# Even fold's row on GpSimd and ScalarE, earlier folds, V's and the norm's parts at other steps, and a first up product inside the attention loop

## The chip, the cores and the metric

One core of one Trainium2 chip. The metric is device time in microseconds (us) from one launch to its end. Matrix products run on TensorE (PE), the rest on VectorE (DVE), ScalarE (ACT) and GpSimd (POOL); SyncE (SP) issues nearly all transfers. Each engine works through its own queue in order and waits on semaphores for the others.

## The reference

Three blocks in a row, two batches of 768 tokens, float32:

```python
# 1: cluster attention: 8 heads of 64 per batch
mask = argmax(q_n . c_n)[:, None] == argmax(k_n . c_n)[None, :]
scores = where(mask, q @ k.T / 8, -1e9)
x = softmax(scores) @ v                      # heads side by side: 768 x 512
# 2: Fourier mixing, norm, MLP
u = x + real(fft(fft(x, axis=tokens), axis=features))
un = (u - mean(u)) / sqrt(var(u) + 1e-6)
x = u + relu(un @ w_ch1) @ w_ch2             # 512 -> 2048 -> 512
# 3: gated convolution MLP
h = relu(x @ w_in)                           # 512 -> 1024
out = (h * sigmoid(conv3(h))) @ w_out
```

## The kernel before, in words

Products keep float32 accuracy by splitting each operand into a high and a low part and multiplying three times (`pass3`).

**Attention.** 16 pairs of batch and head are cut into 6 blocks of 128 queries, 96 blocks in all. One loop runs over the step n from -8 to 105 (L791 to 815). At step n it issues, in this order: what the dictionary `pre` holds for n; the s products of block n+8 and, on VectorE, their maximum (`score_max`, L552 to 571), with `mid` between the two; the high part of block n-1's probabilities (`prob_hi`); the t products of block n and their exponential on ScalarE (`score_exp`); the low part of n-1 (`prob_lo`), on VectorE for the blocks in `LO_ON_DVE`, else on GpSimd; the products of block n-3 with V (`attn_v`); then `aft`, `post` and `fill`. `at(where, n, f)` puts further work into these five. The order of this loop is written by hand (`manual_schedule`): every engine's queue holds exactly the sequence that the steps issue. From block 88 on the odd blocks (`IN_PLACE`) keep their probabilities in PSUM.

Score tiles are three slots of two PSUM banks in rotation (`slot`, L356). A product waits until the slot's last reader is done, most often the maximum, the exponential, or an in-place low part.

For a pair m of heads (8 pairs) `prep_*` picks clusters and builds stacked operands (its 24 cluster products, `prep_sims`, are issued at step 12m-19), and `v_*` scales V: `load_v` (a transfer into the one tile `vraw`), `v_max` (magnitude, VectorE), `v_turn` (a product that turns it), `v_step` 0 to 3 (small, VectorE), 4 (scaled copy, ScalarE) and 5 (the residual, VectorE).

Inside the loop run also, for batch 0: the mixing (`mixing`, table `plan` L702 to 709), whose even fold adds mirrored halves (`even0`, `even1`), takes a row of 257 differences on one partition (`row`, L131 to 137, into rows 0 and 32 of `Zx`), then sums and splits (`even`, `evenH`, `evenL`); the norm (`norm`, L713 to 720), six token tiles in five parts each; conversions of two weight blocks ahead (`ahead_*`); and the split of the first weight block (`first_split`).

**MLPs.** After the loop the program is no longer ordered by hand: a planner sorts each engine's queue by the readiness that it computes, and may draw such work into the loop's idle time. `mlp1_up(0, 0)` is the first up product, of 2 halves with 12 products each; `load_w` brings a weight block as 64-bit words (tile `raw64`, two buffers) and converts it with four VectorE operations and one of ScalarE (`from64`); `squares` sums squares of a block on ScalarE and overwrites its raw tile, for blocks 0 and 1 in two `junk` tiles of the same two buffers. `later` issues batch 1's mixing as a side line of the first MLP.

Of the kernel before, what the change touches and what calls it, by code (L numbers as in the profile page):

```python
# [24 lines left out]
LO_ON_DVE = ({n for n in range(54) if n % 12 in (2, 7, 8, 10)}  # L25
             | {n for n in range(54, 87) if n % 12 in (1, 2, 7, 11)} | {87})

# [22 lines left out]
def tile_net(ctx, tc, qk, v, cen, w12, w34, conv, dft, odd, out):  # L50
# [3 lines left out]
    def f32(ap):  # L54
        return ap.bitcast(F32)
# [39 lines left out]
    def mixing(b, bank, bank2, low, other):  # L95
# [35 lines left out]
        @stage("row")  # L131
        def _():
            r1 = dp.tile([1, N2], F32, tag="row", bufs=1, name=f"r1{b}")
            ev = d["ev", 0], d["ev", 1]
            V.tensor_sub(r1[:, 0:257], ev[0][0:1, 0, 0:257], ev[1][0:1, 0, 0:257])
            V.tensor_copy(Zx[0:1, 0:257], r1[:, 0:257])
            V.tensor_sub(Zx[32:33, 0:257], r1[:, 0:257], f32(Zx[0:1, 0:257]))

# [173 lines left out]
    def load_w(k, f):  # L312
        w = place_w(k, f)
        raw = cvs[0].tile([128, 2048], I32, tag="raw64", bufs=2, name=f"raw{k}{f}")
        nc.sync.dma_start(out=raw.bitcast(I64), in_=(w12 if k == "a" else w34)[f])
        for op in from64(w, raw):
            op()
        squares(k, f, raw[:, 0:256].bitcast(BF16))

# [28 lines left out]
    with ExitStack() as actx:  # L348
# [7 lines left out]
        def slot(name):  # L356
            turn[0] = (turn[0] + 1) % 3
            return ps.tile([128, 2, 512], F32, tag=f"s{turn[0]}", bufs=1, name=name)
# [301 lines left out]
        def at(where, step, *f):  # L660
            where.setdefault(step, []).append(f)

        for m in range(1, NH // 2):
            k = 12 * m - 24
            if m > 1:
                at(pre, k, load_raw, m)
                at(post, k + 5, prep_sims, m)
                at(fill, k + 6, prep_first, m)
                at(fill, k + 7, prep_pick, m)
                at(fill, k + 8, prep_hi, m, (0,))  # L670
                at(fill, k + 9, prep_lo, m, 0, G)
                at(fill, k + (9 if m < 7 else 8), prep_hi, m, (1,))
                at(mid, k + 11, prep_turn, m)
                at(fill, k + (10 if m < 7 else 9), prep_lo, m, 1, G)
            at(fill, k + 14, load_v, m)
            at(aft, k + 17, v_max, m)
            at(mid, k + 19, v_turn, m)
            for i in range(4):
                at(aft, k + 19, v_step, m, i)
            at(fill, k + 24, v_step, m, 4)  # L680
            at(fill, k + 25, v_step, m, 5)
        at(fill, -8, prep_first, 1)
# [3 lines left out]
        at(fill, 0, stack_mask, 2)  # L686
        at(fill, 0, v_step, 0, 5)
        at(pre, -2, first_max, 0)
# [8 lines left out]
        def two(name):  # L697
# [3 lines left out]
        first = mixing(0, lambda name: slot(name)[:, 0], two, V, G)  # L701
        plan = (("even0", fill, 54), ("even1", fill, 55), ("row", aft, 57), ("even", fill, 58), ("evenH", aft, 59),  # L702
                ("evenL", fill, 59),
                ("odd0", fill, 60), ("y0", post, 61), ("odd1", fill, 61), ("y0L", pre, 62), ("y1", post, 62),
# [9 lines left out]
        for i, t in enumerate((0, 3, 1, 4, 2, 5)):  # L714
            n = 73 + 3 * i
            at(fill, n, stat, t)
            at(pre, n + 1, root, t)
            at(aft, n + 2, scale, t)
            at(post, n + 3, swap, t)
            at(pre, n + 4, low, t)  # L720

# [19 lines left out]
        for i, t in enumerate((Zx, Zy, YcH[:, :, N1:512], YcL[:, :, N1:512])):  # L741
            at(fill, 4 + i, V.memset, f32(t), 0.0)
        for q in range(AHEAD):
            at(pre, AHEAD_STEPS[5 * q] - 3, ahead_start, q)
            at(pre, AHEAD_STEPS[5 * q + 4] + 1, ahead_store, q)
# [12 lines left out]

        at(fill, 92, first_split, 0)
        at(fill, 93, first_split, 1)  # L760
        at(fill, 95, first_split, 2)
        at(fill, 97, first_split, 3)

# [92 lines left out]
    def mlp1_up(g, f):  # L856
        if (g, f) == (0, 0):
            h = hs[0, g, f] = [dp.tile([128, 780], F32R, tag=t, bufs=1, name=f"first{t}")[:, 0:S] for t in ("e0", "e1")]
            w = ws[0, g, f]
        else:  # L860
            if g:
                t = hp.tile([128, S], F32R, tag="hH", bufs=3, name=f"h{g}_{f}").bitcast(F16)
                h = hs[0, g, f] = [t[:, 0:S], t[:, S:2 * S]]
                w = ws[0, g, f] = split_16(hp, "a", f) if f == 0 else ws[0, g, f]
            else:
                h = hs[0, g, f] = [hp.tile([128, S], F32R, tag=t, bufs=3, name=f"{t}{g}_{f}") for t in ("hH", "hL")]
                w = ws[0, g, f] = split_w(hp, 3, "a", f, f"a{g}_{f}", V)
        for i in range(2):
# [145 lines left out]
    side = later()  # L1014
    mlp1_up(0, 0)
    for f in range(2):
        squares("a", f, cvs[0].tile([128, 2048], I32, tag="raw64", bufs=2, name=f"junk{f}")[:, 0:256].bitcast(BF16))
    load_w("a", 2)
# [110 lines left out]
```

## Time and profile before

| | us |
|---|---|
| median of 3 runs | 701.67 (700.02 to 703.91) |
| profiled execution, its span | 702.69, 700.9 |
| PE busy | 667.3 (95%) |
| DVE busy | 543.9 (78%) |
| ACT busy | 410.8 (59%) |
| POOL busy | 200.3 (29%) |

The profile is of one execution, so a sum made from its rows is to be compared with 702.69. A busy PE is not PE at its peak: matmuls overlap, and a lower granted clock makes each longer. The attention loop fills the span from 15 to 282 us; the first MLP follows, then the second.

### The profile page before, as it was taken

What the parts mean: (1) busy time and instruction counts of PE and PEld (TensorE: products, weight loads), DVE (VectorE), ACT (ScalarE), POOL (GpSimd) and SP (SyncE); (2) the same over time, 40 slices, a digit from 0 to 9 for tenths busy, and PEclk for the clock granted to TensorE, in tenths of its full rate; (3) what the DMA queues carried; (4) which work ended last, traced back from release to release, by engine and by line L of the source; (5) the groups of instructions that cost most, each with busy time, mean ns of one, the idle gap of its engine ahead of it and who ended that gap; (6) DMA issues with size and microseconds to landing.
All of it is one profiled execution on the core that took longest, in us unless ns stands there. A gap on an engine that the chain in (4) does not pass through costs nothing.

```text
span 700.9 us, 12789 instructions
## 1 busy us (share of the span) xinstructions
PE 667.3 (95%) x5106; PEld 504.6 (72%) x5106; DVE 543.9 (78%) x873; ACT 410.8 (59%) x664; POOL 200.3 (29%) x168
## 2 busy tenths in 40 slices
PE   8799999998899997989999999999999999999997
PEld 6598988987799886869998998555555555555553
DVE  7777889898877997999469976997634399867662
ACT  3478869787458787536335654676534367555442
POOL 8156658568646945121041000000000000000000
PEclk9999999999899999999999999999999999999999
DMA  7747696773633413224203350243000000001002
GB/s 219 198 110 193 158 244 157 213 209 84 155 87 78 106 62 122 68 98 144 113 0 121 121 180 10 77 156 122 0 2 1 1 0 1 1 1 71 20 1 90
DMA packets 22087, 66.50 MB, mean 95 GB/s; under 512 B 4502, under 2 KB 7562, under 8 KB 19212
## 3 DMA queue, kind: packets, MB, share of 16 engines
q1 hardware_dynamic: 21020, 61.94, 31.0%
q0 software_dynamic: 1008, 3.75, 2.0%
q8 instruction: 40, 0.66, 0.4%
q14 instruction: 19, 0.16, 0.1%
HBM read 40.94 MB, written 5.77 MB: 67 GB/s over the span
## 4 chain that ended last, share of the span: by engine, by line
PE 72%; DVE 16%; DMA 4%; issue 2%; ACT 2%; POOL 2%; SPq 1%; DVEq 0%; ACTq 0%; POOLq 0%
PE acc L86 8%; PE acc L87 8%; PE acc L85 8%; PE up L85 5%; PE up L87 5%; PE up L86 5%; PE av L641 5%; PE s L566 3%; PE t L601 3%; PE s L568 3%; PE t L603 3%; DVE m L571 3%; PE sim L440 3%; PE u L85 2%; PE u L87 2%
## 5 line engine op out<-in xcount | busy, mean ns | idle before, releaser
L629 POOL TENSOR_TENSOR p<-p,p 128x768 f16<-128x768 f32 x62 | 107.5, 1735 | 85.7 <-ACT p L621 59.5
L571 DVE TENSOR_REDUCE m<-s 128x1 f32<-128x768 f32 x96 | 90.5, 947 | 13.8 <-PE s L568 6.5
L609 ACT ACTIVATE p<-t,cbias 128x768 f32<-128x768 f32 x92 | 82.8, 900 | 26.2 <-PE t L603 25.0
L621 ACT CAST p<-p 128x768 f16<-128x768 f32 x88 | 73.0, 830 | 1.2
L641 PE MATMUL av<-V,p 128*128 128x65 f16 x1728 | 70.8, 195 | 2.8 <-POOL p L629 2.8
L641 PEld LDWEIGHTS <-p 128*128 128x128 f16 x1728 | 59.3, 99 | 18.3 <-issue 15.1
L601 PE MATMUL t<-X 128*128 128x384 f32 x192 | 54.5, 365 | 8.6 <-DVE m L571 6.9
L566 PE MATMUL s<-X 128*128 128x384 f32 x192 | 56.2, 374 | 3.2 <-DMA X<-ohd 1.8
L568 PE MATMUL s<-Y 96*128 96x384 f32 x192 | 50.0, 341 | 1.1 <-DMA Y<-G 1.1
L603 PE MATMUL t<-Y 98*128 98x384 f32 x192 | 50.2, 343 | 0.0
L85 PE MATMUL up<-un,wha 128*128 128x384 f32 x120 | 41.3, 344 | 2.7 <-DVE YcL L163 1.3
L85 PE MATMUL u<-x,wb 128*128 128x384 f16 x128 | 41.7, 326 | 1.3 <-DVE h L892 0.9
L87 PE MATMUL up<-un,wla 128*128 128x384 f32 x120 | 40.5, 338 | 1.8 <-DVE wla L853 1.8
L601 PEld LDWEIGHTS t<-X 128*128 128x128 f32 x192 | 32.0, 192 | 13.9 <-issue 6.7
L85 PE MATMUL up<-un,wa 128*128 128x384 f16 x128 | 41.7, 326 | 0.0
L87 PE MATMUL up<-un,wa 128*128 128x384 f16 x128 | 41.7, 326 | 0.0
L86 PE MATMUL up<-un,wa 128*128 128x384 f16 x128 | 41.7, 326 | 0.0
L87 PE MATMUL u<-x,wb 128*128 128x384 f16 x128 | 41.7, 326 | 0.0
L86 PE MATMUL u<-x,wb 128*128 128x384 f16 x128 | 41.7, 326 | 0.0
L86 PE MATMUL up<-un,wha 128*128 128x384 f32 x120 | 40.5, 338 | 0.0
L629 DVE TENSOR_TENSOR p<-p,p 128x768 f16<-128x768 f32 x30 | 37.7, 1257 | 0.1
L85 PE MATMUL acc<-wb,gH 128*128 128x512 f16 x96 | 36.4, 379 | 0.5 <-ACT gH L900 0.5
(368 smaller groups left out, 1701.0 us busy)
## 6 DMA issues: line engine op xcount, KB each, us to landing
rawa<-w SPq DMA_DIRECT2D x14, 1024.0 KB
rawb<-w SPq DMA_DIRECT2D x8, 1024.0 KB
raw<-qk SPq DMA_DIRECT2D x7, 768.0 KB
X<-G SPq DMA_DIRECT2D x14, 384.0 KB
Y<-G SPq DMA_DIRECT2D x14, 384.0 KB
vraw<-v SPq DMA_DIRECT2D x8, 384.0 KB
out<-y SPq DMA_DIRECT2D x12, 256.0 KB
X<-G SPq DMA_DIRECT2D x14, 192.0 KB
```

Of the source, the lines that this page charges most:

```text
L85: T.matmul(o, sH, mH, start=start, stop=False)
L86: T.matmul(o, sH, mL, start=False, stop=False)
L87: T.matmul(o, sL, mH, start=False, stop=stop)
L566: T.matmul(t[:, c, 0:384], X[:, 0, sl], X[:, 1, 384 * c:384 * c + 384], start=True, stop=False)
L568: T.matmul(t[:, c, 0:384], Y[0:96, 0, sl], Y[0:96, 1, 384 * c:384 * c + 384], start=False, stop=True)
L571: V.tensor_reduce(m6s[h][:, i:i + 1], t[:, :, 0:384], AX.XY, ALU.max, negate=True)
L601: T.matmul(t[:, c, 0:384], X[:, 1, sl], X[:, 0, 384 * c:384 * c + 384], start=True, stop=False)
L603: T.matmul(t[:, c, 0:384], Y[0:98, 1, sl], Y[0:98, 0, 384 * c:384 * c + 384], start=False, stop=True)
L609: A.activation(p, t[:, :, 0:384], AF.Exp, bias=cbias, scale=0.125)
L621: A.copy(p16[:, 0], p32s[n])
L629: eng.tensor_sub(p16[:, 1], p, p16[:, 0])
L641: T.matmul(o, p16[:, k, 128 * j:128 * j + 128], v16[:, i, h % 2, 65 * part:65 * part + 65], start=(i + j + k + part == 0), stop=(i == 5), ...
```

## The change

- `row` is four stages: a subtraction on GpSimd, a copy on ScalarE (`rowH`), a second subtraction on GpSimd (`rowL`), a copy on ScalarE (`rowZ`). In batch 0 they stand at steps 54, 56, 56 and 58; `even0` and `even1` move from 54 and 55 to 52 and 53. In batch 1 they follow each other.
- V's parts of pair m: the load at 12m-17 (before 12m-10), the magnitude at 12m-12 (12m-7), its turn and the small steps at 12m-10 (12m-5), the scaled copy and the residual at 12m-7 (12m and 12m+1), the step that issues the next pair's cluster products. The first pair's stand at 0, 4, 5 and 5, the last pair's copy and residual at 78 and 79.
- The norm's five parts all move one step later.
- `first_split` is at 91 to 94 (92 to 97). The first up product is issued at steps 96 and 97 in two halves, from slots of the loop, ahead of the products of blocks 94 and 95 with V.
- The low part of block 94 moves to VectorE.
- The squares of weight blocks 0 and 1 are taken with those of blocks 4 and 5, over their raw tiles.

```diff
-             | {n for n in range(54, 87) if n % 12 in (1, 2, 7, 11)} | {87})
+             | {n for n in range(54, 87) if n % 12 in (1, 2, 7, 11)} | {87, 94})
...
         @stage("row")
         def _():
-            r1 = dp.tile([1, N2], F32, tag="row", bufs=1, name=f"r1{b}")
-            ev = d["ev", 0], d["ev", 1]
-            V.tensor_sub(r1[:, 0:257], ev[0][0:1, 0, 0:257], ev[1][0:1, 0, 0:257])
-            V.tensor_copy(Zx[0:1, 0:257], r1[:, 0:257])
-            V.tensor_sub(Zx[32:33, 0:257], r1[:, 0:257], f32(Zx[0:1, 0:257]))
+            r1 = d["r1"] = dp.tile([1, N2], F32, tag="row", bufs=1, name=f"r1{b}")
+            G.tensor_sub(r1[:, 0:257], d["ev", 0][0:1, 0, 0:257], d["ev", 1][0:1, 0, 0:257])
+        @stage("rowH")
+        def _():
+            A.copy(Zx[0:1, 0:257], d["r1"][:, 0:257])
+        @stage("rowL")
+        def _():
+            G.tensor_sub(d["r1"][:, 0:257], d["r1"][:, 0:257], f32(Zx[0:1, 0:257]))
+        @stage("rowZ")
+        def _():
+            A.copy(Zx[32:33, 0:257], d["r1"][:, 0:257])
...
-        squares(k, f, raw[:, 0:256].bitcast(BF16))
+        for i in (f, f - 4) if k == "a" and f in (4, 5) else (f,):
+            squares(k, i, raw[:, 0:256].bitcast(BF16))
...
-            at(fill, k + 14, load_v, m)
-            at(aft, k + 17, v_max, m)
-            at(mid, k + 19, v_turn, m)
+            first = m == 1
+            at(fill, 0 if first else k + 7, load_v, m)
+            at(aft, 4 if first else k + 12, v_max, m)
+            at(mid, 5 if first else k + 14, v_turn, m)
             for i in range(4):
-                at(aft, k + 19, v_step, m, i)
-            at(fill, k + 24, v_step, m, 4)
-            at(fill, k + 25, v_step, m, 5)
+                at(aft, 5 if first else k + 14, v_step, m, i)
+            at(aft, k + 17 + (m == 7), v_step, m, 4)
...
-        at(fill, 0, v_step, 0, 5)
+        fill[0].insert(0, (v_step, 0, 5))
...
-        plan = (("even0", fill, 54), ("even1", fill, 55), ("row", aft, 57), ("even", fill, 58), ("evenH", aft, 59),
-                ("evenL", fill, 59),
+        plan = (("even0", fill, 52), ("even1", fill, 53), ("row", fill, 54), ("rowH", aft, 56), ("rowL", fill, 56),
+                ("even", fill, 58), ("rowZ", fill, 58), ("evenH", aft, 59), ("evenL", fill, 59),
...
-            at(fill, n, stat, t)
+            at(fill, n + 1, stat, t)
...
+        for m in range(1, NH // 2):
+            at(aft, 12 * m - 7 + 2 * (m == 7), v_step, m, 5)
...
+        def first_up(i):
+            if i == 0:
+                hs[0, 0, 0] = [dp.tile([128, 780], F32R, tag=t, bufs=1, name=f"first{t}")[:, 0:S] for t in ("e0", "e1")]
+            h, tk = hs[0, 0, 0], slice(384 * i, 384 * i + 384)
+            o = slot(f"up0_{i}")[:, 0, 0:384]
+            up_half(o, ws[0, 0, 0], uns[0], i)
+            A.activation(h[0][:, tk], o, AF.Relu)
+            V.scalar_tensor_tensor(h[1][:, tk], o, 0.0, f32(h[0][:, tk]), ALU.max, ALU.subtract)
-        at(fill, 92, first_split, 0)
-        at(fill, 93, first_split, 1)
-        at(fill, 95, first_split, 2)
-        at(fill, 97, first_split, 3)
+        at(fill, 91, first_split, 0)
+        at(fill, 92, first_split, 1)
+        at(fill, 93, first_split, 2)
+        at(fill, 94, first_split, 3)
+        at(post, 96, first_up, 0)
+        at(post, 97, first_up, 1)
...
-    mlp1_up(0, 0)
-    for f in range(2):
-        squares("a", f, cvs[0].tile([128, 2048], I32, tag="raw64", bufs=2, name=f"junk{f}")[:, 0:256].bitcast(BF16))
     load_w("a", 2)
```

## Rows read from the trace of the kernel before

**Rows 1.** The page's first part: engine, busy us, share, instructions.
```profile
PE 667.3 (95%) x5106; PEld 504.6 (72%) x5106; DVE 543.9 (78%) x873; ACT 410.8 (59%) x664; POOL 200.3 (29%) x168
```

**Rows 2.** Timeline at block 59: start us, us, engine, line, operation, shapes [idle before <-releaser].
```profile
169.49 1.85 POOL L115 TENSOR_TENSOR ev<-U 128x765 f32<-128x765 f32 x1
...
171.37 1.85 DVE L135 TENSOR_TENSOR r<-ev,ev 1x257 f32<-1x257 f32 x1 [1.13 <-POOL ev L115]
...
175.06 1.74 DVE L137 TENSOR_TENSOR Zx<-r,Zx 1x257 fp32r<-1x257 f32 x1
...
178.18 0.98 PE L601 MATMUL t<-X 128*128 128x384 f32 x2 [5.34 <-DVE m L571]
```

**Rows 3.** Stretches: us, then each engine's busy us (count), PE's clock, DMA share, GB/s.
```profile
156.00:181.00 25.00, 19.59 (x218) 17.66 (x215) 20.82 (x29) 15.39 (x22) 22.35 (x16) 0.92 0.40 101
...
178.00:184.00 6.00, 5.83 (x45) 5.24 (x46) 4.74 (x7) 2.73 (x4) 4.36 (x4) 0.51 0.71 154
225.00:262.00 37.00, 35.50 (x424) 31.57 (x423) 36.36 (x64) 30.68 (x44) 26.48 (x20) 1.00 0.39 96
```

**Rows 4.** Timeline: GpSimd's first and last low part, and block 58's product.
```profile
156.01 3.31 POOL L629 TENSOR_TENSOR p<-p,p 128x768 f16<-128x768 f32 x2 [3.47 <-ACT p L621]
...
178.44 2.49 POOL L629 TENSOR_TENSOR p<-p,p 128x768 f16<-128x768 f32 x1
...
185.62 0.73 PE L641 MATMUL av<-V,p 128*128 128x65 f16 x18
```

**Rows 5.** Groups on GpSimd, 156 to 181 us: count | busy us, mean ns | idle before.
```profile
L629 POOL TENSOR_TENSOR p<-p,p 128x768 f16<-128x768 f32 x7 | 12.8, 1824 | 6.0 <-ACT p L621 3.5 <-issue 2.6
```

**Rows 6.** Timeline: the other batch's row, and a one-partition copy on ScalarE.
```profile
297.13 0.41 DVE L135 TENSOR_TENSOR r<-ev,ev 1x257 f32<-1x257 f32 x1
...
320.29 0.46 ACT L158 CAST Zy<-y 1x386 fp32r<-1x386 f32 x1
```

**Rows 7.** PE's waits, 55 to 155 us: in total, times, longest.
```profile
PE t L601 <- DVE m L571: 1.2, 3, 0.5
PE s L568 <- DMA Y<-G: 1.1, 2, 0.9
```

**Rows 8.** Groups of V's parts, whole span: count | busy us, mean ns | idle before.
```profile
L548 DVE SCALAR_TENSOR_TENSOR V<-vraw,vsc,V 128x768 f16<-128x768 f32 x8 | 11.7, 1457 | 0.0
...
L525 DVE TENSOR_REDUCE vsc<-vraw 128x1 f32<-128x768 f32 x8 | 7.6, 947 | 2.9 <-DMA vraw<-v 2.9
L546 ACT ACTIVATE V<-vraw,vsc 128x768 f16<-128x768 f32 x8 | 7.4, 927 | 0.6 <-DVE vsc L544 0.6
```

**Rows 9.** Timeline: the maximum of step 4 and the t products of step 5.
```profile
36.70 0.93 DVE L571 TENSOR_REDUCE m<-s 128x1 f32<-128x768 f32 x1
...
38.07 0.52 PE L601 MATMUL t<-X 128*128 128x384 f32 x2
```

**Rows 10.** PE's waits, 262 to 286 us, and VectorE's in-place low parts there.
```profile
PE av L641 <- POOL p L629: 2.8, 2, 1.6
PE t L601 <- DVE d L649: 1.2, 1, 1.2
...
L627 DVE TENSOR_TENSOR p<-t,p 128x768 f16<-128x768 f32 x4 | 3.8, 958 | 2.9 <-ACT p L617 2.9
```

**Rows 11.** Timeline: from the last attention product to block 1's up product.
```profile
280.49 1.05 ACT L851 CAST wha<-wa 128x1024 fp32r<-128x1024 f32 x1 [2.42 <-PE av L641]
...
281.45 1.28 DVE L299 TENSOR_SCALAR wa<-rawa 128x1024 int32<-128x1024 int32 x2
...
283.78 1.22 DVE L853 TENSOR_TENSOR wla<-wa,wha 128x1024 fp32r<-128x1024 f32 x1
...
285.52 0.44 PE L85 MATMUL up<-un,wha 128*128 128x384 f32 x1 [0.76 <-DVE firste L874]
```

**Rows 12.** PE's waits, 281 to 315 us.
```profile
PE up L87 <- DVE wla L853: 1.8, 1, 1.8
PE up L85 <- DVE YcL L163: 1.3, 1, 1.3
```

More of the change, by code (lines that the diff above doesn't have):

```diff
@@ L715, in tile_net @@
             n = 73 + 3 * i
-            at(fill, n, stat, t)
[L717 to L720, printed above, removed]
+            at(fill, n + 1, stat, t)
+            at(pre, n + 2, root, t)
+            at(aft, n + 3, scale, t)
+            at(post, n + 4, swap, t)
+            at(pre, n + 5, low, t)
         ahead, wdr = {}, [dr.tile([128, 1024], F32, tag=f"w{f}", bufs=1, name=f"wdr{f}") for f in range(AHEAD // 2)]
@@ L856, in mlp1_up @@
     def mlp1_up(g, f):
-        if (g, f) == (0, 0):
-            h = hs[0, g, f] = [dp.tile([128, 780], F32R, tag=t, bufs=1, name=f"first{t}")[:, 0:S] for t in ("e0", "e1")]
-            w = ws[0, g, f]
-        else:
[L861 to L867, printed above, removed]
+        if g:
+            t = hp.tile([128, S], F32R, tag="hH", bufs=3, name=f"h{g}_{f}").bitcast(F16)
+            h = hs[0, g, f] = [t[:, 0:S], t[:, S:2 * S]]
+            w = ws[0, g, f] = split_16(hp, "a", f) if f == 0 else ws[0, g, f]
+        else:
+            h = hs[0, g, f] = [hp.tile([128, S], F32R, tag=t, bufs=3, name=f"{t}{g}_{f}") for t in ("hH", "hL")]
+            w = ws[0, g, f] = split_w(hp, 3, "a", f, f"a{g}_{f}", V)
         for i in range(2):
```

## The prediction

> **What bounds the kernel now.** I read the page's first part, then the waits of TensorE stretch by stretch, then the timeline around the longest of them. TensorE is busy 667.3 of 700.9 us [rows 1], so an edit pays only where TensorE waits or runs slowly. The longest wait is at block 59 of the attention loop: 5.34 us in which the t products stand still until VectorE has freed a slot with a maximum [rows 2]. VectorE was late because of the even fold's row. Its first subtraction sat 1.13 us until GpSimd had folded the second half (169.49 plus 1.85), and then the three operations on one partition took 1.85 us, as much again, and 1.74, although the same subtraction of the other batch takes 0.41 [rows 2, 6]: GpSimd was running beside them. [...] The other waits are small: 2.3 us between 55 and 155 us, mostly for VectorE and a stack's transfer [rows 7]; 37.0 - 35.5 = 1.5 us in 225 to 262, where VectorE is busy 36.4 of 37.0 [rows 3]; 2.8 + 1.2 us at the attention's end and 0.8 after it [rows 10, 11]; 1.8 + 1.3 us early in the first MLP [rows 12].
>
> **The change part by part.** All sums are against the profiled execution: 702.69 us, with a span of 700.9. The median of the runs is 701.67, so 1.0 us comes off at the end.
>
> *Row and even folds.* VectorE loses three operations at step 57 and no longer waits there; GpSimd gains two subtractions on 257 elements, ScalarE two copies. The trace has no such operation on GpSimd. From below, three-element operations take 0.2; from above, 765 elements take 1.85 [rows 2]; in proportion 257 elements take 0.75, and I take 1.5 for two. ScalarE's nearest is 0.46 for a copy of 386 elements on one partition [rows 6]; two cost 0.9 at most, and hide in the time that ScalarE stands idle there (busy 15.4 of the 25.0 us from 156 to 181) [rows 3]; where it falls behind, the three slots take up as much. The stall therefore goes, and GpSimd is late next. Its queue from step 52 is the low parts of blocks 51 to 54 and 56 to 58, the two folds, the cluster pick's product, two subtractions for the next pair's operands and now the row, all in order. In 156 to 181 us it is busy 22.35 us [rows 3], and it starts at 156.01 [rows 4], when block 51's high part is there. The fold put at step 52 finds its last head's output ready at that time, so GpSimd runs without a pause: 156.0 + 22.35 + 1.5 = 179.9 us for the low part of block 58. Its product can run then; in the trace it begins at 185.62 [rows 4]. That is 5.7 us gained. [...] Lower bound: the seven low parts average 1.82 [rows 5], and the longest takes 2.49 [rows 4]; at 2.49 each, 4.7 us more, the gain is 1.0. I stay at 5.7 because the 22.35 us already hold the collisions with VectorE of today. The pick on VectorE, too, waits for its product, now behind a fold and a low part; the maximum queued behind it frees a slot late, inside that same wait.
>
> [...]
>
> *V's parts.* The scaled copy (0.93, ScalarE) and the residual (1.46 on VectorE, mean of eight, stretched beside GpSimd) leave steps 12m and 12m+1, where VectorE is full, for step 12m-7, whose 24 cluster products leave it slack; the magnitude (0.95) goes the other way, and its 2.9 us of waiting for V's transfer [rows 8] should end, since the load is issued five steps ahead of it and not three. On SP the load stands between a stack's moves and the next maxima instead of behind the raw load, so the burst that held back a Y move (0.9 of the 1.1 us) is smaller. Of the 2.3 us [rows 7] I count 1.9 as gone. New costs: at step 5 the first pair's magnitude ends at 36.70 + 0.93 + 0.95 = 38.6, and the product that turns it stands ahead of a t product that began at 38.07 [rows 9]: 0.5 us. In the product steps the residual now waits 0.93 for ScalarE, and the weight conversion and the cluster maxima queue behind it on VectorE: 0.2 us in each of three, 0.3 at most (estimates). Net gain 0.8; bounds 2.3 gained and 1.4 lost.
>
> *Norm's parts one step later, V's magnitude of the last pair out of 225 to 262.* VectorE loses 0.95 us of its 36.4 there, so about 0.7 of the 1.5 us goes; between 1.5 gained and 0.5 lost, should a shifted statistic meet a low part.
>
> *The attention's end.* Block 94's low part goes from GpSimd to VectorE and two up products fill TensorE while it is made, so the later of GpSimd's two waits, 1.6, goes. The first, 1.2, stays: the norm's statistic no longer stands ahead of block 88's high part, but block 91's scores now take the slot that block 89 keeps in place until its low part is done. Of the 1.2 for a slot [rows 10] 0.9 goes, since the last transposition's copy is behind the high part on ScalarE. The 0.8 after the first up product [rows 11] goes. Against that a cover is lost. The copy of block 1's weights waits 2.42 us for the last attention product, as its place is free only then, and now no up product follows that one: the copy (1.05) and the subtraction (1.22) are bare [rows 11], 2.3 us. Gain 1.6 + 0.9 + 0.8 - 2.3 = 1.0. Bounds: 3.3, if the split hides; a loss of 1.3, if block 2's conversions still stand ahead of that subtraction on VectorE, as they do from 281.45 to 283.78 [rows 11].
>
> *First MLP.* For the second batch VectorE loses three row operations of about 0.4, and ScalarE's copy of the even half stands behind a chain GpSimd, ScalarE, GpSimd, ScalarE, some 0.4 us late. The four deferred squares are hidden by ScalarE's idle half there, and the raw tiles come free sooner, so conversions may start earlier. I count 0.7 of the 3.1 us [rows 12] as gained; bounds 3.1 gained, 2 lost, since a planner orders this part anew.
>
> Sum: 5.7 + 0.8 + 0.7 + 1.0 + 0.7 = 8.9 us; 702.7 - 8.9 = 693.8, and 1.0 less for the median: **692.8 us**.
>
> **The rivals.** *GpSimd becomes the bound.* Its operations stretch toward 2.49 us beside VectorE's moved residuals, and blocks 57 and 58 wait for their low parts. For it: no pause is left in its queue, and ScalarE feeds it later. Against: the trace's 22.35 us come from the same mix, less the row. [...]
>
> *More than forecast.* The waits left in the first MLP and in the norm's stretch go too, because VectorE is the late engine in both: 2.4 + 0.8 more, and the split of block 1 hides, 2.3: 687.3. Against: each was already counted once in part, and VectorE stays nearly full.
>
> *The other side: the conversions come before the attention's end.* Blocks 2 and 3's raw tiles are no longer held by the squares, so the planner may put their eight conversions (two of 0.64 and six of 1.22, the size of the subtraction [rows 11]: 8.6 us) into VectorE's queue ahead of the last low parts. [...] For it: the planner works by readiness. Against: block 2's place is free only after block 92's low part, and the two up products run beside them.
>
> [...]
>
> **How the numbers follow.** Forecast 0.58 (own range 689.5 to 696); GpSimd the bound 0.17 (half of it under 698.2); more than forecast 0.11; half the event stays 0.07; conversions early 0.07. A measurement here tells 0.5% from no change, 3.5 us, so faster means under 698.2: 0.58 + 0.11 + 0.09 (GpSimd) + 0.07 (half the event) = 0.85; within 0.5%: 0.08 (GpSimd) + 0.02 (conversions) = 0.10; slower: the conversions' other 0.05. The range leaves out the early conversions, the upper GpSimd cases and the bottom of the gains: 687 to 698.5.
>
> **What would show it.** Right: no wait over 1 us at block 59, full clock from 170 to 190 us, GpSimd busy without a pause up to the low part of block 58, and that block's product at 179 to 180 us less what was gained before; no wait of VectorE's magnitude for V's transfer; a new wait of about 0.5 us at step 5; no wait for GpSimd before block 94's products, and a new one of some 2 us before block 1's up product, ended by its weights' split. Wrong: a wait of over 3 us for a GpSimd low part between blocks 56 and 61, the lower clock anywhere after block 50, or weight conversions between the last blocks' high and low parts on VectorE.

## The result and the profile after

The changed kernel takes 708.54 us (median of four runs, 708.17 to 708.73) against 701.64 before: ratio 1.0095, interval 1.0067 to 1.0124. I had forecast 692.8. The profiled execution took 708.48 us, its span 706.7, 5.8 us more than before's 700.9.

Where those 5.8 us lie is read most quickly from the start of each block's first product on TensorE, in both timelines. A stage's length is the difference of two such starts:

| stage (us) | before | after | after minus before |
|---|---|---|---|
| up to the first scores (step -8) | 15.12 | 16.92 | +1.8 |
| steps -8 to 3 | 19.99 | 19.99 | 0 |
| blocks 4 to 51 | 118.23 | 122.54 | +4.3 |
| blocks 52 to 63 (folds, row) | 42.35 | 40.99 | -1.4 |
| blocks 64 to 91 (norm) | 74.28 | 75.32 | +1.0 |
| block 92 to the last attention product | 10.48 | 12.79 | +2.3 |
| the rest | 420.45 | 418.16 | -2.3 |

The last two rows belong together: the first up product, 24 matmuls in 4.2 us, moved from the one to the other, so the attention's end gained 1.9 and the rest lost 1.9. The 1.8 us at the start come from operations that the change doesn't touch; of sixteen experiments fifteen started the scores at 14.9 to 15.5 us and one, of another kernel, at 16.9, so I take them for chance, which isn't shown: the changed kernel's other three runs took as long, and no profile shows their start.

The first part of the page after, as in [rows 1]:

```profile
PE 667.9 (95%) x5106; PEld 503.6 (71%) x5106; DVE 546.2 (77%) x868; ACT 413.9 (59%) x668; POOL 203.2 (29%) x171
```

Stretches after, columns as in [rows 3]; the first two are some 7 us later than those of before, as the whole loop is:

```profile
163.00:188.00 25.00, 21.28 (x245) 18.67 (x243) 20.63 (x25) 19.43 (x28) 24.64 (x18) 1.00 0.44 104
184.00:190.00 6.00, 5.17 (x56) 4.21 (x56) 5.68 (x6) 4.97 (x7) 6.00 (x4) 1.00 0.79 190
229.00:266.00 37.00, 35.02 (x417) 31.70 (x414) 35.31 (x59) 28.95 (x40) 25.86 (x19) 1.00 0.51 145
```

The wait of 5.34 us at block 59 is gone and the granted clock is 1.00 where it was 0.51 [rows 3]; TensorE is busy 21.3 of 25 us and not 19.6, GpSimd busy 24.6 of 25 us and then without a pause, all as forecast. In the norm's stretch VectorE is 1.05 us less busy, also as forecast, and TensorE is less busy still: the relief bought nothing. The waits of TensorE in the loop, from 57 to 162 us, which are the steps of the stretch of [rows 7]:

```profile
PE t L611 <- DVE m L581: 3.2, 4, 1.2
PE s L585 <- DVE m L581: 2.2, 2, 1.1
PE s L578 <- DMA Y<-G: 2.0, 2, 1.1
```

They were to fall by 1.9 us and grew from 2.3 to 7.4. What made them is seen at blocks 17 to 22 of the timeline after:

```profile
73.17 1.02 DVE L558 SCALAR_TENSOR_TENSOR V<-vraw,vsc,V 128x768 f16<-128x768 f32 x1 [1.51 <-ACT V L556]
...
74.56 0.69 DVE L309 SCALAR_TENSOR_TENSOR ahead<-ahead 128x512 int32<-128x512 int32 x1
...
75.28 0.66 ACT L310 ACTIVATE ahead<-ahead 128x512 f32<-128x512 f32 x1 [2.15 <-DVE ahead L309]
...
76.79 1.66 POOL L639 TENSOR_TENSOR p<-p,p 128x768 f16<-128x768 f32 x1 [3.74 <-issue]
...
78.40 0.92 POOL L460 TENSOR_TENSOR eq<-eq,desc 128x384 f16<-128x384 f16 x1
...
79.28 1.66 POOL L639 TENSOR_TENSOR p<-p,p 128x768 f16<-128x768 f32 x1
...
79.36 0.55 DVE L464 TENSOR_REDUCE m<-eq 128x24 f16<-128x384 f16 x1 [0.91 <-POOL eq L460]
...
79.95 1.41 DVE L466 TENSOR_TENSOR oh<-desc,m 128x384 f16<-128x384 f16 x1
...
82.14 2.56 DVE L639 TENSOR_TENSOR p<-p,p 128x768 f16<-128x768 f32 x1
...
82.28 0.61 PE L611 MATMUL t<-X 128*128 128x384 f32 x2 [0.66 <-DVE m L581]
...
85.69 0.27 PE L585 MATMUL s<-ident,m 128*6 128x128 f32 x1 [1.09 <-DVE m L581]
```

The residual (L558) waits 1.51 us for ScalarE's copy, the weight conversions stand behind it, ScalarE's square (L310) waits for those, the next block's high part stands behind the square, and GpSimd's low part behind that. Counted from block 17's first product, the square starts 5.58 us in and not 4.40, GpSimd's low part 7.09 and not 5.93. VectorE then waits 0.91 for the cluster pick's product, and its next operation (L466), 0.56 long before, starts 0.67 after a GpSimd low part and takes 1.41. Its low part takes 2.56, beside another GpSimd operation, and TensorE waits twice for a maximum, 0.66 and 1.09 us.

TensorE's waits after, from 270 to 293 us, around the attention's end, as in [rows 10] (L637 is VectorE's in-place low part):

```profile
PE t L611 <- DVE p L637: 2.0, 2, 1.6
```

The same view from 289 to 345 us, early in the first MLP, as in [rows 12]:

```profile
PE up L87 <- DVE wla L876: 3.7, 2, 2.6
PE up L85 <- DVE YsL L198: 1.7, 1, 1.7
```

The wait for GpSimd before block 94's products is gone, block 91's wait for the in-place low part of block 89 came (1.6), and the first MLP waits more than before.

### The profile page after: what moved, and what is told of

It reads as the page before. It is cut to its first block, busy times and chain, and to the rows that moved or that the text cites. A ratio compares the mean times of both kernels' runs of the same rounds, so it can differ in the third digit from the quotient of the medians.

```text
span 706.7 us, 12788 instructions
## 1 busy us (share of the span) xinstructions
PE 667.9 (95%) x5106; PEld 503.6 (71%) x5106; DVE 546.2 (77%) x868; ACT 413.9 (59%) x668; POOL 203.2 (29%) x171
## 4 chain that ended last, share of the span: by engine, by line
PE 63%; DVE 23%; issue 4%; ACT 3%; DMA 3%; POOL 3%; SPq 1%; DVEq 0%; POOLq 0%; ACTq 0%
PE acc L87 7%; PE acc L86 7%; PE acc L85 7%; PE up L85 5%; PE up L87 5%; PE up L86 5%; DVE m L581 4%; PE av L651 4%; PE t L611 3%; PE s L576 3%; PE t L613 2%; DVE p L639 2%; PE s L578 2%; PE u L85 2%; PE u L87 2%
## 5 line engine op out<-in xcount | busy, mean ns | idle before, releaser
L639 POOL TENSOR_TENSOR p<-p,p 128x768 f16<-128x768 f32 x61 | 105.4, 1729 | 93.5 <-ACT p L631 58.3
L639 DVE TENSOR_TENSOR p<-p,p 128x768 f16<-128x768 f32 x31 | 38.5, 1243 | 0.4 <-ACT p L631 0.3
L578 PEld LDWEIGHTS s<-Y 96*128 96x128 f32 x192 | 35.3, 191 | 2.6 <-issue 2.6
```

The source lines that it names most:

```text
L578: T.matmul(t[:, c, 0:384], Y[0:96, 0, sl], Y[0:96, 1, 384 * c:384 * c + 384], start=False, stop=True)
L639: eng.tensor_sub(p16[:, 1], p, p16[:, 0])
```

## The experiments

Times are medians. The kernel before took 702.21 us beside the first four, 701.90 beside the next eight, 702.12 and 701.84 beside the last.

**Each part alone.** Four kernels: before plus one part.

```diff
+("even0", fill, 52), ("even1", fill, 53), ("row", fill, 54), ("rowH", aft, 56), ("rowL", fill, 56), ... ("rowZ", fill, 58)   # row_only
+at(aft, k + 17 + (m == 7), v_step, m, 4)  ...  at(aft, 12 * m - 7 + 2 * (m == 7), v_step, m, 5)   # v_only
+at(fill, n + 1, stat, t)  ...  at(pre, n + 5, low, t)   # norm_only
+at(post, 96, first_up, 0)  ...  LO_ON_DVE ... | {87, 94}   # tail_only
```

> The kernel before with the row's new parts and the folds from step 52 alone; V's parts, the norm's parts and the attention's end as before. Theory (V's parts cost what the change lost, the row's part paid): the wait of 5.34 us at block 59 and the lower clock behind it go, 7.2 us less in steps 59 and 60, and new waits of some 3.5 us at blocks 57 to 62 give half of it back: 696.5 to 699, 3 to 5 us under before. Rival (GpSimd is overfilled by the folds and the row, and that alone is the loss): no gain, 701 to 705, with the waits of 1.4 to 1.5 us at blocks 54 and 57 all there. Rival (my forecast of this part was right by itself): 695 to 697.

> The kernel before with V's parts alone in their new steps. Theory (V's residual waits in the product steps for ScalarE's copy, and the late conversions make high part, low part and cluster pick collide with GpSimd): about 0.8 us lost at step 5, 1 us at each of blocks 21, 22, 45, 46, 38, 1.6 at 54 and 2 to 3 at blocks 80 to 84, 6 to 8 us in all: 706 to 709, slower than before. Rival (the losses come from the row's and the norm's parts and from chance collisions at the start): 700 to 702. Forecast of this part by itself: 700.9.

> The kernel before with the norm's five parts one step later alone. Theory: V's last magnitude and residual, not the norm, fill VectorE at blocks 80 to 84, so this part by itself is worth little: 701 to 702.5, within 0.7 us of before. Rival (the shifted statistics meet low parts and GpSimd): 702.5 to 704, a loss of 1 to 2 us between 230 and 265 us of the span.

> The kernel before with the attention's end alone: block 94's low part on VectorE, block 0's up product among the last products with V, its squares later. Theory: the end of the attention gains about 2 us (the wait of 1.6 before block 94's products goes), and the first MLP gives it back in waits for the low parts of its weights (2.6 us at one place): 700.5 to 703. Rival (forecast of this part): 699.5 to 700.5. Rival (the tail is the loss): 703 to 706.

| part | us | ratio (interval) |
|---|---|---|
| row and even folds | 702.59 | 1.0011 (0.9992 to 1.0031) |
| V's parts | 709.89 | 1.0123 (1.0103 to 1.0143) |
| norm's parts | 704.15 | 1.0043 (1.0017 to 1.0068) |
| attention's end | 699.57 | 0.9973 (0.9956 to 0.9991) |

The sum is 0.4 + 7.7 + 1.9 - 2.6 = 7.4 us beside the 6.9 of the whole. V's parts are the loss, the norm's a second one, the attention's end gains 2.6 where I had given it 1.0 (its interval, 0.6 to 3.1, holds both), and the row, which was to bring 5.7 us, brings nothing that can be told from no change. None of the four landed in its theory's range: the row missed my 3 to 5 us (its rival's 701 to 705 held, but not its reason, GpSimd), V's parts cost 0.9 more and the norm's 1.7 more than the top of what I expected, and the attention's end came out as in the forecast of it, 699.5 to 700.5, and not by the theory that the first MLP gives it back.

In the row's run the wait at block 59 does go: blocks 59 and 60 are 8.0 us shorter (I had put 5.3 on the wait and 2.9 on the clock behind it), and the low part of block 58 ends at 178.47 + 1.66 = 180.1 us (179.9 forecast). But that block's product comes only at 182.69, behind a wait of 1.62 for a maximum of VectorE, and blocks 54, 57, 58 and 61 are 0.5, 1.8, 1.5 and 3.5 us longer. From its timeline:

```profile
158.32 1.08 DVE L308 TENSOR_SCALAR ahead<-ahead 128x512 int32<-128x512 int32 x1
...
159.07 1.83 POOL L638 TENSOR_TENSOR p<-p,p 128x768 f16<-128x768 f32 x1
...
159.43 2.02 DVE L309 SCALAR_TENSOR_TENSOR ahead<-ahead 128x512 int32<-128x512 int32 x1
...
166.58 2.10 DVE L465 TENSOR_TENSOR oh<-desc,m 128x384 f16<-128x384 f16 x1
...
166.62 1.64 POOL L638 TENSOR_TENSOR p<-p,p 128x768 f16<-128x768 f32 x1
...
168.22 1.04 POOL L142 TENSOR_TENSOR r<-r,Zx 1x257 f32<-1x257 f32 x1
...
169.41 1.65 POOL L638 TENSOR_TENSOR p<-p,p 128x768 f16<-128x768 f32 x1
...
169.47 2.41 DVE L638 TENSOR_TENSOR p<-p,p 128x768 f16<-128x768 f32 x1
...
169.60 0.61 PE L610 MATMUL t<-X 128*128 128x384 f32 x2 [1.66 <-DVE m L580]
...
178.47 1.66 POOL L638 TENSOR_TENSOR p<-p,p 128x768 f16<-128x768 f32 x1
...
181.87 0.62 PE L610 MATMUL t<-X 128*128 128x384 f32 x2 [1.62 <-DVE m L580]
...
182.69 0.73 PE L650 MATMUL av<-V,p 128*128 128x65 f16 x18
...
183.63 2.14 DVE L311 SCALAR_TENSOR_TENSOR ahead<-ahead 128x512 uint32<-128x512 uint32 x1
```

In blocks 52 to 62 the row's three operations take 5.37 us off VectorE, and seven others (the low parts counted as one) grow by 7.1: L308 0.48 to 1.08, L309 0.69 to 2.02, L465 0.80 to 2.10, the low parts by 0.72, the even half's sum 0.94 to 1.66, L126 0.96 to 1.92, L311 0.68 to 2.14. With smaller differences VectorE's operations add up to 36.1 us in the 38.0 of these blocks, where they added up to 34.9 in 38.5 (neighbours overlap a little; the profile's windows have it busy 34.5 and 33.5): it was the late engine before, and it stays so.

Nor did all of the lower clock go. Columns as in [rows 3]:

```profile
171.00:177.00 6.00, 5.80 (x55) 4.78 (x53) 5.34 (x9) 4.48 (x9) 5.21 (x4) 0.73 0.02 4
```

As an estimate, TensorE's busy time times the missing share of the clock, that is 5.80 x 0.27 = 1.6 us, where the same product of [rows 3] is 5.83 x 0.49 = 2.9. It is paid two blocks earlier, behind the wait of 1.66 at block 57.

**The row's parts and the folds taken apart.** First the row on GpSimd and ScalarE with the folds at their old steps (shown against the row's run), then the early folds with the row on VectorE (against the kernel before).

```diff
-("even0", fill, 52), ("even1", fill, 53), ("row", fill, 54), ("rowH", aft, 56), ("rowL", fill, 56),   # row_54
+("even0", fill, 54), ("even1", fill, 55), ("row", fill, 56), ("rowH", aft, 58), ("rowL", fill, 58),
...
-plan = (("even0", fill, 54), ("even1", fill, 55), ("row", aft, 57), ...   # row_dve
+plan = (("even0", fill, 52), ("even1", fill, 53), ("row", aft, 57), ...
```

> The row's four parts on GpSimd and ScalarE as in the change, but the folds at their old steps 54 and 55 and the row's parts two steps later (56, 58, 58, 60). Theory A (the fold from step 52 runs beside the two weight conversions, 1.08 and 2.02 us in place of 0.48 and 0.69, and so makes ScalarE's square, the high part and the pick late): the waits at blocks 54 and 57 (0.4 and 1.7 us) go, the one at 59 stays gone, 698 to 700. Theory B (VectorE is the bound of blocks 53 to 63, and what leaves it comes back as longer operations beside GpSimd, wherever the folds stand): 701 to 703, with waits in other places of the same sum.

> The folds from step 52 as in the change, but the row's three operations on VectorE at step 57 as before. Theory A (the early folds cost 3 us by the conversions, the row's move pays): the waits at blocks 54 and 57 come, and of the event at block 59 the 1.1 us for the fold go, the three long operations stay: 703 to 706. Theory B (VectorE's sum decides): the three take 0.4 to 0.6 each where no GpSimd operation runs, 1.8 where one does; 701 to 704. Rival (the early fold alone would have done it): 695 to 698.

706.64 us (1.0068, 1.0047 to 1.0089) and 699.02 us (0.9973, 0.9948 to 0.9997): I had them the wrong way round, and the rival on the second, that the early fold alone would have done it, came nearest. Of the 5.7 us for the row and the folds, 2.9 belong to the folds (interval 0.2 to 3.6), which spare VectorE the wait for GpSimd. TensorE's waits in that run, from 152 to 190 us:

```profile
PE t L601 <- DVE m L571: 3.9, 2, 2.9
```

The longest, at block 59, is 2.90 us and not 5.34. The row's move gives this back: by the medians it costs 3.6 us beside the early folds and 4.7 beside the old ones. Why is plainest in the timeline of the kernel with the folds at 54:

```profile
170.74 0.72 POOL L134 TENSOR_TENSOR r<-ev,ev 1x257 f32<-1x257 f32 x1
...
171.43 1.64 POOL L638 TENSOR_TENSOR p<-p,p 128x768 f16<-128x768 f32 x1
...
171.82 9.47 DVE L151 TENSOR_TENSOR ev<-ev,ev 128x771 f32<-128x771 f32 x1
...
173.03 1.82 POOL L508 TENSOR_TENSOR G<-raw,G 128x768 fp32r<-128x768 f32 x1
...
174.82 1.62 POOL L638 TENSOR_TENSOR p<-p,p 128x768 f16<-128x768 f32 x1
...
176.41 1.79 POOL L506 TENSOR_TENSOR G<-raw,G 128x768 fp32r<-128x768 f32 x1
...
178.17 0.72 POOL L142 TENSOR_TENSOR r<-r,Zx 1x257 f32<-1x257 f32 x1
...
178.85 1.62 POOL L638 TENSOR_TENSOR p<-p,p 128x768 f16<-128x768 f32 x1
...
182.22 1.01 PE L610 MATMUL t<-X 128*128 128x384 f32 x2 [7.64 <-DVE m L580]
```

A sum of 0.94 us starts 0.39 after a GpSimd operation and ends 0.82 after the last of six that follow one another without a gap: 9.47 us. None of the six is longer for it: the low parts take 1.62 to 1.64 us and the operations on G 1.79 and 1.82, where in the kernel before most take 1.64 to 1.68 and 1.81 to 1.86. The maximum behind it frees the slot for which TensorE waits 7.64 us.

**The same sum on GpSimd.**

```diff
-V.tensor_add(ev[0][:, :, 0:257], ev[0][:, :, 0:257], ev[1][:, :, 0:257])
+(V if b else G).tensor_add(ev[0][:, :, 0:257], ev[0][:, :, 0:257], ev[1][:, :, 0:257])
```

> The row's four parts on GpSimd and ScalarE with the folds at 54 and 55 (706.6 us), and the even half's sum on GpSimd too in place of VectorE, where it took 9.47 us. Theory (VectorE's two-input operations and GpSimd's exclude each other; the sum started 0.4 us after a GpSimd operation and got its turn only 0.8 us before its end, when six GpSimd operations in a row were done): on GpSimd it takes 1.7 to 2, VectorE goes on, the wait of 7.6 us at block 60 goes: 699 to 702. Rival (the sum waited for something else, the row's chain or a transfer): the wait moves to GpSimd and 705 to 708 stay.

705.44 us: the rival's number by neither's reason. The sum takes 1.80 us on GpSimd, and with the folds at 54 the second of its two inputs was done at 170.66, before it started on VectorE, so the profile leaves nothing but GpSimd that can have held it up there. But on GpSimd it starts only at 182.37, behind five of the same six operations, and the wait of 6.1 us moves to block 61. GpSimd's backlog bounds that place here: on VectorE the sum stands behind it much as it does in GpSimd's own queue. The profiled execution took 709.19 us, the slowest of this kernel's; blocks 52 to 63 took 44.8 us in it, and as much with the sum on VectorE.

**V's parts, place by place.** From v_only on: the copy earlier (v_early); a looser placing of everything (v_fit); v_early with the magnitude a step later (v_both); that with the last pair's copy at step 78, where the change has it (v_both7).

```diff
-at(aft, k + 17 + (m == 7), v_step, m, 4)
+at(aft, k + 17 if first else k + 15, v_step, m, 4)                      # v_early
...
-at(aft, 4 if first else k + 12, v_max, m)
+at(aft, 4 if first else k + 13, v_max, m)                               # v_both, and v_fit
...
+at(aft, k + 17 if first else k + 18 if m == 7 else k + 15, v_step, m, 4)   # v_both7
...
+at(mid, 6 if first else k + 15, v_turn, m)                              # v_fit
+at(aft if m == 1 else fill, 7 if m == 1 else 12 * m - 7, v_step, m, 5)
```

> V's parts alone as in the changed kernel, but ScalarE's scaled copy two steps earlier (12m-9 in place of 12m-7; three steps earlier for the last pair), so that the residual behind it on VectorE finds it done; the first pair as in the changed kernel. Theory (the residual's wait of 1.5 us for the copy delays the weight conversions, ScalarE's square behind them, the high part behind that and so GpSimd's low part and the cluster pick, which then collide): the residual takes the place of the magnitude that left, the conversions start as early as before, and the waits at blocks 21, 22, 34, 45, 46 and 57 (7.0 us in the sum of their steps with V's parts alone) go: 702 to 704, about 6 to 7 us under the 709.9 of V's parts alone. Rival (the residual itself, a two-input operation beside GpSimd, is too much for those steps, whenever its copy is made): 707 to 710.

> V's parts alone, placed so that no conversion stands behind them on VectorE: the magnitude a step later (12m-11), the product and the scales at 12m-9, the copy at 12m-8, the residual at 12m-7 behind the conversions and not ahead of them; for the first pair product and copy at step 6, residual at 7. Theory (the loss of 7.7 us is the order in VectorE's queue: residual ahead of the conversions, magnitude ahead of another one): the waits at blocks 21, 38, 45, 50 and 57 go, 701 to 703. Rival (any two-input operation or magnitude put into those steps meets GpSimd somewhere): 706 to 710.

> V's parts alone with the copy two steps earlier and the magnitude one step later (12m-11, ahead of its product at 12m-10), so that neither the residual waits for the copy nor the weight conversion at step 12m-12 stands behind the magnitude. Theory (the loss is the order in VectorE's queue, place by place): the waits of 1.2 us at blocks 38 and 50 and part of those at 80 and 82 go too, 704 to 706. Rival (an operation moved away from one meeting with GpSimd meets it in the next, since GpSimd and VectorE are both filled): 707.5 to 710, with as much waiting in other blocks.

> V's parts alone with the copy two steps earlier and the magnitude one step later, as the run before, but the last pair's copy at step 78, where the change has it. Theory (the loss is a sum of single meetings): blocks 64 to 92 take 74.8 us again and not 76.8, the last pair's residual 1.0 us and not 2.0, and the whole 706 to 707.5. Rival (a meeting taken away comes back elsewhere): 708.5 to 710.

| kernel | us | ratio (interval) | blocks 4 to 51 | 52 to 63 | 64 to 91 |
|---|---|---|---|---|---|
| before | 701.9 | | 118.2 | 42.4 | 74.3 |
| v_only | 709.89 | 1.0123 (1.0103 to 1.0143) | 122.6 | 44.6 | 74.8 |
| v_early | 708.84 | 1.0104 (1.0084 to 1.0124) | 120.7 | 43.6 | 76.6 |
| v_fit | 709.48 | 1.0101 (1.0075 to 1.0128) | 120.4 | 43.3 | 74.9 |
| v_both | 708.80 | 1.0104 (1.0079 to 1.0129) | 119.9 | 43.5 | 76.8 |
| v_both7 | 706.12 | 1.0057 (1.0039 to 1.0075) | 121.1 | 43.6 | 74.9 |

The stages are of one profiled execution each; for the five V kernels these took 710.48, 708.59, 705.67, 712.12 and 709.58 us. With the copy early the waits at blocks 22, 34 and 46 went, and with them some 1.27 us each, as the chain of waits above has it; the total hardly moved. Three of my four expectations missed, and in all three the rival's range held: what is moved away from one meeting of VectorE and GpSimd comes into another. New waits of 1.2 us stood at 38 and 50, where the magnitude pushed a conversion into GpSimd's low parts (0.68 to 2.11 us), and 1.8 us came in blocks 64 to 91. Curing the first gave half of it back to a wait for the magnitude itself (0.6 at 26, 38, 50). The second is one meeting, a two-input operation of VectorE at the same time as one of GpSimd. The last pair's residual (L548) and GpSimd's low part (L629) in the timeline of v_only:

```profile
250.94 1.00 DVE L548 SCALAR_TENSOR_TENSOR V<-vraw,vsc,V 128x768 f16<-128x768 f32 x1
...
251.12 2.34 POOL L629 TENSOR_TENSOR p<-p,p 128x768 f16<-128x768 f32 x1 [1.25 <-ACT p L621]
```

And in that of v_early, where VectorE's next low part follows:

```profile
246.70 1.65 POOL L629 TENSOR_TENSOR p<-p,p 128x768 f16<-128x768 f32 x1 [0.57 <-ACT p L621]
...
247.21 1.96 DVE L548 SCALAR_TENSOR_TENSOR V<-vraw,vsc,V 128x768 f16<-128x768 f32 x1
...
251.55 2.17 DVE L629 TENSOR_TENSOR p<-p,p 128x768 f16<-128x768 f32 x1
```

The residual that starts 0.18 before the low part takes 1.00, and the low part 2.34; the one that starts 0.51 after takes 1.96, and the low part 1.65. In v_both7 the residual starts 0.17 before a low part again (1.01), blocks 64 to 91 take 74.9, and the whole 706.12, as the theory had it. This meeting, worth 2.7 us between v_both and v_both7, had come in with v_early; v_only's 74.8 don't hold it. v_both7 still takes 4.3 us more than the kernel before beside it, so 3.4 of the 7.7 us could be taken away. The rest lies in step 5 (0.8), in waits such as those for the magnitude, and in blocks 52 to 63 (1.3); these I did not take apart.

**Parts together.** The change without V's parts (e_noV), and versions meant to beat both kernels: the attention's end with V's parts re-timed (best1); the attention's end with the early folds (best2); that with the row's copy on ScalarE (best3), or with the norm's first stage shifted (best4).

```diff
+at(mid, 6 if first else k + 14, v_turn, m)  ...  at(aft, 6 if first else k + 15, v_step, m, 4)   # best1
+plan = (("even0", fill, 52), ("even1", fill, 53), ("row", aft, 57), ...                          # best2
+("row", aft, 57), ("rowH", aft, 57), ("rowL", fill, 58),                                         # best3
+at(fill, n + 0 + (i == 0), stat, t)  ...  at(pre, n + 4 + (i == 0), low, t)                          # best4
```

> The whole change but V's parts, which stay as before. Theory (the parts add: 0.4 for the row, 1.9 for the norm, 2.6 gained at the attention's end): 701.6, 700.5 to 703. Rival (the row's and the norm's losses come from V's parts beside them): 694 to 698.

> The attention's end as in the change, V's parts with the copy two steps earlier, and the first pair's product one step later (its scales and copy at step 6, its residual at 7), so that the product doesn't wait for the magnitude; row, folds and norm as before. Theory: 2.6 us gained at the attention's end, V's parts worth between 1 lost and 1.5 gained: 698 to 700.5. Rival (the residual is too much in any case): 703 to 707.

> The attention's end of the change and its folds from step 52, with the row on VectorE as before, V's parts and the norm as before. Theory (the parts add, as the four single ones did: 0.4 + 7.7 + 1.9 - 2.6 = 7.4 beside the 6.9 of the whole change): 702 less 2.6 for the end and 2.9 for the early folds, 696.5, range 695 to 698. Rival (the early folds' gain was a lucky order that another phase loses): 699 to 701.

> The kernel with the change's attention's end and early folds, and of the row's three operations the middle one, the copy (1.81 us on VectorE with the early folds), on ScalarE, the two subtractions on VectorE, the second at step 58. Theory (VectorE is the late engine up to block 60, and a copy on ScalarE takes 0.4 and meets nobody): 0.5 to 1.5 us under the same kernel with the copy on VectorE, 695 to 696. Rival (the second subtraction then starts inside a run of GpSimd operations and waits for its end, as the sum of the even half did for 9.47 us with the folds at 54): 700 to 706.

> The attention's end of the change, its folds from step 52 with the row on VectorE, and of the norm's six stages only the first one step later. Theory (the first stage's shift took away the wait of 0.65 us at block 76 and 0.8 us in blocks 76 to 80 in the kernel with the norm's parts alone; the later stages lost it at 83 to 90, where V's residual then took 2.42 us beside GpSimd): 0.5 to 1 us under the same kernel without it, 697.7 to 698.2. Rival (one shift moves what stands behind it as well): 699 to 700.5.

e_noV took 704.74 us (1.0031, 1.0009 to 1.0053), 3 us over the sum of its parts, a gap that their intervals hardly settle. From the last attention product on it takes 418.2 us, as the change does, where the attention's end alone takes 416.4 (best1 416.1, best4 416.4, best2 417.6): the row's four stages of the second batch seem to cost up to 1.7 there, which no run tests alone. In its profiled execution V's magnitude at block 41, back in its old place, waits 3.69 us for V's transfer, block 42 is some 2 us longer than before, and the granted clock is 0.66 from 134 to 139 us (0.991 over the run, 0.994 over that of before). The kernel of the sum on GpSimd shows the same (3.62 and some 2), best2 a part of it (2.58 and 0.9); how often it happens stays open. best1 took 707.64 us (1.0084, 1.0065 to 1.0103), over even its rival's range. best2 took 698.73 us (0.9953, 0.9935 to 0.9971) and beats both kernels, 2.2 us behind the sum of its parts, which the intervals don't settle; best3, 698.70 us (0.9954, 0.9935 to 0.9974), cannot be told from it: its wait at block 59 falls from 2.89 to 0.55 and one of 2.59 comes at block 60, where the even half's sum now takes 2.48. best4, 699.41 us (0.9964, 0.9942 to 0.9986), gains nothing: block 76 is 1.95 us shorter, block 77 is 2.31 longer.

## Why the prediction was wrong

The parts were to bring 8.2 us together and cost 7.4, each timed alone: V's parts make 8.5 of that miss, the row and the folds 6.1, the norm 2.6, and the attention's end came out 1.6 better.

**The row and the folds (5.7 forecast, 0 measured).** The wait at block 59 went as forecast. With the row alone GpSimd's low part of block 58 ended within 0.3 us of the forecast, in part by luck (GpSimd began 0.6 us earlier and paused for 0.8), and 1.6 of the 2.9 us for the clock were paid elsewhere; in the whole change the clock's part came out. The step that failed is "The stall therefore goes, and GpSimd is late next", and with it "Its product can run then": VectorE was late next, and the product of block 58 ran 2.6 us after its low part, behind a maximum of VectorE. I took three operations off it at their full length and left the lengths of all others as they were, because "the 22.35 us already hold the collisions with VectorE of today". They hold GpSimd's side of them. VectorE's side I had read for the row alone, 1.85 and 1.74 us beside GpSimd where the other batch's first subtraction takes 0.41 [rows 2, 6], and did not price for the operations that come to stand beside GpSimd in its place. The GpSimd rival was half right: in the changed kernel low parts did stretch, to 2.30 to 2.38 us, and block 58's ended 29.0 us after the first product of step 52 and not 26.5. But TensorE waited for VectorE's maxima there too, 2.3 us from 159 to 192 us, and not for a low part.

The chances of three rivals (GpSimd the bound; half the event stays, the event being the wait at block 59 and the clock behind it; conversions early) rest on prices with 2.9 us for that clock, all or half of it. That was my estimate, and no run shows the term. What the kernel before shows is the same run of products, from a block's t products to the second s products after them, at both clocks:

```profile
163.67 0.59 PE L601 MATMUL t<-X 128*128 128x384 f32 x2
...
167.06 0.60 PE L566 MATMUL s<-X 128*128 128x384 f32 x2
...
184.12 0.59 PE L566 MATMUL s<-X 128*128 128x384 f32 x2
```

At 1.00 it takes 167.06 - 163.67 = 3.39 us; from the t products at 178.18 [rows 2], at 0.53, it takes 5.94, 2.55 us more.

**V's parts (0.8 gained forecast, 7.7 lost).** The bounds were 2.3 and -1.4. Step 5 was right (0.5 forecast, 0.8 measured). What failed is "0.2 us in each of three": I saw the conversions queued behind the residual on VectorE, and did not follow them to ScalarE's square, the high part behind it and GpSimd's low part. The 1.5 us travelled through three engines and ended as collisions. V's wait for its transfer did end, but in the profiled execution of the kernel before TensorE had not been waiting there.

**The norm (0.7 gained forecast, 1.9 lost alone).** A gain of 2.0 us at block 76 came, and losses of 1.3 to 1.8 at blocks 77, 83, 86 and 90, where shifted operations met low parts (V's residual 1.01 to 2.42 us at 257 us of that run, the scaling L269 up to 1.71, beside 0.54); one is block 91's wait for the in-place low part (1.66), which I had put into another term; behind it the granted clock is 0.72 from 270 to 276 us, with TensorE busy 5.48 (0.989 over the run, 0.994 over that of before). The step that failed is the bound, 0.5 lost "should a shifted statistic meet a low part": the scaling and V's residual met them too.

**The attention's end (1.0 forecast, 2.6 alone, 0.6 to 3.1).** Right in kind. The term that was mis-sized is the bare split of block 1: the wait for its low part after is 1.04 us and not 2.3.

**First MLP (0.7 gained forecast, 1.9 lost after the moved product is taken out).** 2.6 us for a weight block's low part and 1.7 for a low part of the mixing stand in place of [rows 12]. That the row's new stages changed the planner's order is the likeliest cause, since the attention's end alone lost 0.2 there and e_noV 1.9; it isn't shown. The bound, 2 lost, held.

## What to carry to other kernels

Where VectorE and GpSimd are both nearly full, an operation taken off one of them is not its length gained: add up what the others on VectorE become when their neighbour on GpSimd moves. Here 5.37 us taken off came back as 7.1. Before moving an operation that waits, list what is queued behind it on its engine, and follow that list over the next two engines to the next operation on VectorE or GpSimd that the trace shows longer beside the other one (here the low parts on VectorE, 0.95 us alone and 1.65 on average when started inside a GpSimd operation). Time each part by itself: here a gain of 2.9 us and one of 2.6 lay hidden under losses of 7.7 and 1.9.

## What the hardware showed

The split by what GpSimd was doing as a VectorE operation started, in the attention loop of the kernel after:

| VectorE operation | no GpSimd operation during it | started inside one |
|---|---|---|
| low part, two inputs in SBUF | 16, 0.94 to 0.96 us | 13, mean 1.65, up to 2.57 |
| maximum, one input in PSUM | 20, 0.94 to 0.96 us | 53, mean 0.95, up to 0.96 |
| V's magnitude, one input in SBUF | | 8, 0.93 to 0.95 us |

Operations during which a GpSimd operation started are left out. Before it is the same: the low parts take 0.95 against 1.61, the maxima 0.95 in both columns. Each of the 13 low parts ends 0.81 to 0.82 us after the GpSimd operation that it started in; in the kernel before there are 14, and they end 0.78 to 0.82 us after it. The row's copy, with one input in SBUF, was longer too (1.81 us for 257 elements in the run with early folds alone, 0.28 for the other batch in the kernel before), and so was the scaling (1.71 beside 0.54).

What I had not expected is that such an operation doesn't always get its turn after one GpSimd operation: the sum of 9.47 us ended 0.82 after the last of six in a row, while in the kernel before each of the row's operations ended 0.15 to 0.28 us after a single one. For the first two, beside [rows 2]:

```profile
171.28 1.66 POOL L629 TENSOR_TENSOR p<-p,p 128x768 f16<-128x768 f32 x1
...
172.88 2.00 POOL L499 TENSOR_TENSOR G<-raw,G 128x768 fp32r<-128x768 f32 x1
...
173.25 1.78 DVE L136 CAST Zx<-r 1x257 fp32r<-1x257 f32 x1
```

In the changed kernel the same sum, started 0.38 us into a GpSimd low part, ended 0.82 after that one: it takes 2.09 us, and GpSimd's next operation 2.54. What decides that isn't shown by any run here.
